# Doubling the K and V items of a streaming decode kernel to 4 MB, with b2 fetched late on the same queue

## The chip, the cores and the metric

The kernel runs on one core of one Trainium2 chip. PE is its matrix engine, ACT and DVE its scalar and vector engines, and SP issues the DMAs of the stream. SBUF is the on-chip memory, in 128 partitions; PSUM is where PE's results land. 16 DMA engines share each load; a packet is one contiguous run that one of them moves, in the trace's records. The metric is device microseconds of one execution; lower is better. Executions of one kernel agree within about 0.1% here. Ratios are the mean time of one kernel's fast runs over that of the other's of the same rounds, so they are not quite the ratios of the medians that stand beside them.

## The reference

One decode step (one query token, batch 2) of a block with adaptive layer norm: a modulation from `c`, grouped-query attention over a cache of 32768 rows, and an MLP. Cut to what matters:

```
mod = silu(c) @ w_mod                       # w_mod 1024 x 6144
h = layernorm(x) * (1 + ca) + sa
q = h @ wq                                  # 32 heads of 128, 4 KV heads, so 8 heads share one K and V
p = softmax(q @ k.T * 128**-0.5)            # k_cache, v_cache: 2 x 4 x 32768 x 128 bf16, 64 MiB each
x = x + ga * ((p @ v) @ wo)
h = layernorm(x) * (1 + cb) + sb
x = x + gb * (gelu(layernorm(h) @ w1 + b1) @ w2 + b2)
```

Everything is bf16 in memory. K and V are 134 of the 178 MB that have to be read. (The sizes of items and runs below are counted in powers of two: an item of 2 MB is 2048 KB.)

## The kernel before

All large inputs form one list of items, in the order of use, and one queue (SP's) fetches them into a ring of 160 KB a partition. An item is issued once what lay in its place has been read.

```python
CH_ROWS = 8192                 # rows of K or V in an item: 64 rows of 256 B a partition
TPC = CH_ROWS // 128
VLAG = 5                       # V item n is fetched after K item n + 5
RING = 160 * 1024
...
    b1T = sb("b1T", [128, FT])
    b2T = sb("b2T", [128, KT8])             # 8 fp32: 32 bytes a partition
    sgT = sb("sgT", [128, 2, KT8])
    ...                                     # more small tensors, S_sb, E_sb, KT_sb
    arena = nc.alloc_sbuf_tensor("arena", [128, RING], mybir.dt.uint8)
    abase = nc.lookup_mloc(arena).addr
    ...
        off = stream[-1].off + stream[-1].nbytes      # in add(): the next place in the ring
        if off + nbytes > RING:
            off = 0
    ...
    def kv_src(cache, i, cc):
        ...
        return cache[b, g][r0:r0 + CH_ROWS, :].rearrange("(p t) d -> p t d", p=128)
    ...                                     # in need(): one load an item, on SP's queue
            T.dma("sp", lambda e, dst=dst, src=cur.src: e.dma_start(dst, src), key=f"d_{cur.reg}", writes=[cur.reg], frees=old)
```

For each K item, PE transposes 128x128 tiles, ACT and DVE copy them out of PSUM, PE multiplies them with q; after the last K item of a head group comes the softmax, and PE multiplies V five items late. b2 is fetched at the start on ACT's queue, transposed into `b2T` and used near the end.

## Time and profile before

The median is 431.4 us. The page, in cut form: the span; then the 40 slices' DMA share (tenths) and rate; then the DMA queues with packets, MB and share of the 16 engines' span; then the chain of waits by engine.

```profile
span 429.7 us, 12974 instructions
...
DMA  8999999999999999999999999999999999999992
GB/s 332 432 422 426 433 432 424 432 424 427 427 432 427 426 433 429 427 433 426 426 432 426 430 433 424 429 432 426 429 429 428 430 429 424 435 424 424 427 386 112
...
q1 hardware_dynamic: 14112, 178.27, 97.6%
q8 instruction: 47, 0.77, 0.6%
...
DMA 70%; PE 24%; ACT 2%; DVE 2%; issue 1%; SPq 1%; ACTq 0%
```

DMA is busy everywhere, at 422 to 435 GB/s from the second slice to the third from the end. PE has time to spare, as the waits view shows (engine, its work, what it waited for: us in total, times, longest):

```profile
PE psKT L546 <- DMA K<-in_A_k_cache_dram: 54.2, 19, 7.5
PE psO L473 <- DMA V<-in_A_v_cache_dram: 9.5, 5, 3.0
```

The end of the stream, in the windows view (stretch and its length, busy time of PE, PE's weight loads, DVE, ACT, POOL, then the granted clock, the DMA share and GB/s):

```profile
414.00:416.00 2.00, 1.10 (x42) 1.02 (x39) 0.00 (x0) 0.00 (x0) 0.00 (x0) 0.50 1.00 422
416.00:418.00 2.00, 0.00 (x0) 0.00 (x0) 0.00 (x0) 0.00 (x0) 0.00 (x0) 0.50 0.76 315
418.00:420.00 2.00, 1.84 (x64) 1.79 (x64) 0.00 (x0) 0.00 (x0) 0.00 (x0) 0.50 0.51 209
422.00:424.00 2.00, 0.69 (x26) 0.70 (x27) 0.00 (x0) 0.00 (x0) 0.00 (x0) 0.50 0.46 193
```

From 418 us the DMA share is 0.5: about half of the DMA engines still have something to move. One load is finished when all engines have counted up its semaphore, and the trace has each count: the first load's counts are 0.4 us apart, the last w2's 9.0 us (416.68 to 425.69). Some engines fall behind during the run, and the stream ends with the slowest. What follows the last landing is short (timeline view: start, duration, engine, line, operation, and in brackets the idle time before it):

```profile
425.74 1.01 PE L591 MATMUL psS<-gT,w 128*128 128x2 bf16 x32 [0.56 <-DMA w<-in_B_w_dram]
427.90 0.37 SPq L603 DMA_DIRECT2D out_dram<-res  x1
```

Durations of single packets on the stream's queue, from the trace's DMA records (these are my own counts over them):

| packet, bytes | used for | packets an engine | median, ns |
|---|---|---|---|
| 7168 | w1 | 64 | 272 |
| 8192 | wq, w2 | 120 | 309 |
| 12288 | w_mod | 64 | 460 |
| 16384 | K, V, wo | 544 | 611 |

That makes 792 data packets an engine.

### The profile page before, as it was taken

The page shows a single profiled execution, that of the slowest core. Times are in us where ns is not written, and L with a number is a line of the kernel's source. Part 1 is how long each engine was busy: PE and PEld are TensorE (multiplying, and loading weights), DVE is VectorE, ACT ScalarE, POOL GpSimd, SP SyncE. Part 2 cuts the span into 40 slices and gives each one's busy share as a digit, 9 for nine tenths or more (in the row PEclk, how much of TensorE's full clock was granted, in tenths as well). Part 3 has the DMA queues.
Part 4 walks back from the last instruction along what each step waited for, and adds up shares of the span by engine and source line. Part 5 has one row for each costly group of instructions (what it writes and reads, how often), then busy time and mean ns, then how long its engine had stood idle before and what let it go on. Part 6 is the DMA issues. An engine that isn't in the chain of part 4 may idle for free.

```text
span 429.7 us, 12974 instructions
## 1 busy us (share of the span) xinstructions
PE 292.2 (68%) x6035; PEld 258.2 (60%) x6035; DVE 162.5 (38%) x344; ACT 158.9 (37%) x266; POOL 1.3 (0%) x9
## 2 busy tenths in 40 slices
PE   0643379859978764997877649777777697535553
PEld 0632379858867663896757548667666585203543
DVE  0200027545665332463543435445434454203200
ACT  1100016575574325362833534446436343500100
POOL 1000000000000000000000000000000000000000
PEclk9999999998989867696996959986988599555555
DMA  8999999999999999999999999999999999999992
GB/s 332 432 422 426 433 432 424 432 424 427 427 432 427 426 433 429 427 433 426 426 432 426 430 433 424 429 432 426 429 429 428 430 429 424 435 424 424 427 386 112
DMA packets 14500, 179.11 MB, mean 417 GB/s; under 512 B 1767, under 2 KB 1774, under 8 KB 2798
## 3 DMA queue, kind: packets, MB, share of 16 engines
q1 hardware_dynamic: 14112, 178.27, 97.6%
q8 instruction: 47, 0.77, 0.6%
q10 hardware_dynamic: 334, 0.02, 0.1%
q14 instruction: 7, 0.06, 0.0%
HBM read 178.28 MB, written 0.00 MB: 415 GB/s over the span
## 4 chain that ended last, share of the span: by engine, by line
DMA 70%; PE 24%; ACT 2%; DVE 2%; issue 1%; SPq 1%; ACTq 0%
DMA K<-in_A_k_cache_dram 50%; PE psKT L546 15%; DMA V<-in_A_v_cache_dram 9%; DMA w<-in_B_w_dram 7%; DMA wmod<-in_w_mod_dram 5%; PE psS L441 4%; PE psO L473 2%; PE psM L510 1%; ACT E_sb L462 1%; SPq L344 1%; PE psM L494 0%; DVE KT_sb L552 0%; PE psM L483 0%; ACT L462 0%; DVE msum L488 0%
## 5 line engine op out<-in xcount | busy, mean ns | idle before, releaser
L546 PE MATMUL psKT<-ident,K 128*128 128x128 bf16 x2048 | 181.1, 240 | 55.1 <-DMA K<-in_A_k_cache_dram 54.2
L546 PEld LDWEIGHTS psKT<-ident,K 128*128 128x128 bf16 x2048 | 138.2, 108 | 70.0 <-DMA K<-in_A_k_cache_dram 63.5
L550 ACT ACTIVATE KT_sb<-psKT 128x1024 bf16<-128x1024 bf16 x96 | 98.3, 1024 | 190.2 <-PE psKT L546 181.3
L552 DVE COPY KT_sb<-psKT 128x1024 bf16<-128x1024 bf16 x160 | 108.2, 689 | 137.7 <-PE psKT L546 137.0
L441 PE MATMUL psS<-qT,KT_sb 128*128 128x8 bf16 x2048 | 91.6, 168 | 7.2 <-ACT KT_sb L550 4.5
L441 PEld LDWEIGHTS psS<-qT,KT_sb 128*128 128x128 bf16 x2048 | 84.0, 100 | 8.6 <-ACT KT_sb L550 4.9
L473 PE MATMUL psO<-V,E_sb 128*32 128x512 bf16 x512 | 38.2, 424 | 10.1 <-DMA V<-in_A_v_cache_dram 9.5
L462 ACT ACTIVATE E_sb<-S_sb,negm 128x256 bf16<-128x256 f32 x64 | 32.5, 508 | 7.0 <-DVE negm L460 5.2
L447 DVE TENSOR_REDUCE m1c<-S_sb 128x8 f32<-128x512 f32 x32 | 22.0, 688 | 14.1 <-ACT S_sb L446 13.0
L473 PEld LDWEIGHTS psO<-V,E_sb 128*32 128x32 bf16 x512 | 11.5, 101 | 22.3 <-DMA V<-in_A_v_cache_dram 13.3
L446 ACT ACTIVATE S_sb<-psS 128x512 f32<-128x512 f32 x32 | 19.0, 594 | 4.4 <-PE psS L441 4.3
L418 PE MATMUL psS<-siluT,wmod 128*128 128x2 bf16 x384 | 11.2, 165 | 8.4 <-DMA wmod<-in_w_mod_dram 6.9
L418 PEld LDWEIGHTS psS<-siluT,wmod 128*128 128x128 bf16 x384 | 10.9, 104 | 8.8 <-DMA wmod<-in_w_mod_dram 7.3
L426 PE MATMUL psS<-hT,wq 128*128 128x2 bf16 x256 | 7.5, 165 | 12.5 <-DMA wq<-in_A_wq_dram 12.5
L426 PEld LDWEIGHTS psS<-hT,wq 128*128 128x128 bf16 x256 | 7.1, 104 | 12.8 <-DMA wq<-in_A_wq_dram 12.8
L591 PE MATMUL psS<-gT,w 128*128 128x2 bf16 x224 | 6.6, 165 | 9.2 <-DMA w<-in_B_w_dram 9.2
L395 ACT ACTIVATE stat<-stat 128x2 f32<-128x2 f32 x3 | 0.6, 203 | 31.8 <-DVE stat L394 31.8
L591 PEld LDWEIGHTS psS<-gT,w 128*128 128x128 bf16 x224 | 6.3, 104 | 9.5 <-DMA w<-in_B_w_dram 9.5
L462 ACT ACTIVATION_READ_ACCUMULATOR E_sb<-S_sb,negm 128x1 f32 x64 | 12.0, 187 | 0.0
L485 DVE RECIPROCAL rinv<-psM 128x1 f32<-128x1 f32 x8 | 1.3, 168 | 22.1 <-PE psM L483 22.1
L573 PE MATMUL psS<-h2T,w 128*128 128x2 bf16 x224 | 7.8, 172 | 2.5 <-DVE x1b L577 1.3
L573 PEld LDWEIGHTS psS<-h2T,w 128*128 128x128 bf16 x224 | 7.6, 118 | 2.6 <-issue 2.6
(86 smaller groups left out, 93.3 us busy)
## 6 DMA issues: line engine op xcount, KB each, us to landing
K<-in_A_k_cache_dram SPq DMA_DIRECT2D x32, 2048.0 KB, 44.2
V<-in_A_v_cache_dram SPq DMA_DIRECT2D x32, 2048.0 KB, 43.2
wmod<-in_w_mod_dram SPq DMA_DIRECT2D x8, 1536.0 KB, 17.2
wq<-in_A_wq_dram SPq DMA_DIRECT2D x4, 2048.0 KB, 37.7
wo<-in_A_wo_dram SPq DMA_DIRECT2D x4, 2048.0 KB, 43.0
w<-in_B_w_dram SPq DMA_DIRECT2D x4, 1792.0 KB, 41.8
w<-in_B_w_dram SPq DMA_DIRECT2D x3, 2048.0 KB, 31.0
w<-in_B_w_dram SPq DMA_DIRECT2D x1, 1024.0 KB, 29.4
```

The source lines that it names most:

```text
L418: pe(lambda e, w=it.view, j=j, k=k: e.matmul(psS[0][:, 2 * j:2 * j + 2], lhsT=w[:, j * 128:(j + 1) * 128], rhs=siluT[:, :, k], start=(k == ...
L426: pe(lambda e, w=it.view, h=h, k=k: e.matmul(psS[1][:, 2 * h:2 * h + 2], lhsT=w[:, k % 2, h * 128:(h + 1) * 128], rhs=hT[:, k, :], start=( ...
L441: pe(lambda e, t=t, jj=jj: e.matmul(ps[:, t * HPG:(t + 1) * HPG], lhsT=KT_sb[kn][:, jj, :], rhs=qT[:, b, g * HPG:(g + 1) * HPG], start=Tru ...
L446: act(lambda e: e.activation(Sc, ps[:, :].rearrange("p (t h) -> p h t", h=HPG), ACT.Copy), reads=[preg], writes=[f"S_sb{i % 2}_{cc}"])
L447: dve(lambda e: e.tensor_reduce(m1c[:, :, cc], Sc, AX.X, ALU.max), reads=[f"S_sb{i % 2}_{cc}"], writes=[f"m1c{cc}"])
L462: act(lambda e, h=h: e.activation(E_sb[j][:, :, h, :], S_sb[j][:, h, :].rearrange("p (u t) -> p u t", t=4), ACT.Exp, bias=negm[j][:, h:h + ...
L473: pe(lambda e, t4=t4, tg=tg, q=q: e.matmul(psO[32 * q:32 * q + 32, :], lhsT=E_sb[j][:, tg // 4, :, :].rearrange("p h t -> p (h t)"), rhs=i ...
L546: pe(lambda e, kq=kq, jj=jj, w=it.view, t=t: e.transpose(psKT[kq][:, jj * 128:(jj + 1) * 128], w[:, t, :], ident[:, :]), reads=[it.reg, "i ...
L550: act(lambda e, kn=kn, src=src: e.activation(KT_sb[kn][:, :, :], src, ACT.Copy), reads=[f"psKT{kq}"], writes=[f"KT_sb{kn}"])
L552: dve(lambda e, kn=kn, src=src: e.tensor_copy(KT_sb[kn][:, :, :], src), reads=[f"psKT{kq}"], writes=[f"KT_sb{kn}"])
L573: pe(lambda e, w=it.view, fc=fc, q=q, j=j, k=k: e.matmul(psS[0][:, 2 * fc:2 * fc + 2], lhsT=w[:, k % 2, q * 512 + j:(q + 1) * 512:4], rhs= ...
L591: pe(lambda e, w=it.view, q=q, j=j, k=k: e.matmul(psS[1][:, 2 * k:2 * k + 2], lhsT=w[:, q % 2, j * DM + k * 128:j * DM + (k + 1) * 128], r ...
```

## The change

The intent is fewer and larger transfers: a partition's share of a K or V item becomes one run of 32 KB, in half as many loads. To keep PSUM and the softmax as they were, the bookkeeping goes by half items. Separately, b2 leaves the head of the kernel and comes just before the last w2 item.

```diff
-CH_ROWS = 8192
+CH_ROWS = 16384
...
-VLAG = 5
+VLAG = 2
...
-    b2T = sb("b2T", [128, KT8])
...
-    T.dma("act", lambda e: e.dma_start(b2m[:, :], B_b2.rearrange("(k p) -> k p", p=128)), key="ld_b2", writes=["b2m"])
...     (the b2 matmul at the head and its copy into b2T go; qk() counts in half items)
+    need("w2", 2)
+    T.dma("sp", lambda e: e.dma_start(b2m[:, :], B_b2.rearrange("(k p) -> k p", p=128)), key="ld_b2", writes=["b2m"])
+    need("w2", 3)
     for q in range(7):
         it = need("w2", q // 2)
+        if q == 6:
+            pe(lambda e: e.matmul(psM[:, 44:52], lhsT=b2m[:, :], rhs=ident[0:KT8, 0:KT8], start=True, stop=True), ...)
+            dve(lambda e: e.tensor_tensor(x1b[:, :, :], mod(5), psM[:, 44:52].unsqueeze(2).to_broadcast([128, KT8, 2]), ALU.mult), ...)
+            dve(lambda e: e.tensor_tensor(x1b[:, :, :], x1b[:, :, :], x1T[:, :, :], ALU.add), ...)
```

More of the change, by code (lines that the diff above doesn't have):

```diff
@@ L30 @@
 NK = NBG * NCH
-VLAG = 5
+STEPS = TPC // 8
+VLAG = 2
 NKT = 6
@@ L263, in bass_adaLN_cond__gqa_block_cached__mixer_channel_mlp__decode_kernel @@
     res16 = sb("res16", [16, 128], BF16)
-    m1c = sb("m1c", [128, HPG, NCH])
+    m1c = sb("m1c", [128, HPG, NT // 64])
     m1 = sb("m1", [128, HPG])
@@ L375, in bass_adaLN_cond__gqa_block_cached__mixer_channel_mlp__decode_kernel @@
         pe(lambda e, j=j: e.matmul(psM[:, 16 + 7 * j:23 + 7 * j], lhsT=b1m[:, j::4], rhs=ident[0:7, 0:7], start=True, stop=True),
-           reads=["b1m", "ident"], writes=["psM"], mark=False)
-    pe(lambda e: e.matmul(psM[:, 44:52], lhsT=b2m[:, :], rhs=ident[0:KT8, 0:KT8], start=True, stop=True),
-       reads=["b2m", "ident"], writes=["psM"])
+           reads=["b1m", "ident"], writes=["psM"], mark=(j == 3))
     dve(lambda e: e.tensor_copy(xT.rearrange("p k b -> p b k"), psM[:, 0:16].rearrange("p (b k) -> p b k", b=2)), reads=["psM"], writes=["xT"])
     dve(lambda e: e.tensor_copy(b1T.rearrange("p (q j) -> p j q", j=4), psM[:, 16:44].rearrange("p (j q) -> p j q", j=4)), reads=["psM"], writes=["b1T"])
-    dve(lambda e: e.tensor_copy(b2T[:, :], psM[:, 44:52]), reads=["psM"], writes=["b2T"])
     def kb(ap2):
@@ L437, in qk @@
         b, g = i % 2, i // 2
-        ps, preg = psS[n % 2], f"psS{n % 2}"
+        hh, half = cc * (TPC // 64) + g8 // 8, (g8 // 8) % 2
+        ps, preg = psS[half], f"psS{half}"
         for jj in range(8):
-            t = g8 * 8 + jj
+            t = (g8 % 8) * 8 + jj
             pe(lambda e, t=t, jj=jj: e.matmul(ps[:, t * HPG:(t + 1) * HPG], lhsT=KT_sb[kn][:, jj, :], rhs=qT[:, b, g * HPG:(g + 1) * HPG],
@@ L443, in qk @@
                reads=[f"KT_sb{kn}", "qT"], writes=[preg], mark=(jj == 7))
-        if g8 == TPC // 8 - 1:
-            Sc = S_sb[i % 2][:, :, cc * TPC:(cc + 1) * TPC]
-            act(lambda e: e.activation(Sc, ps[:, :].rearrange("p (t h) -> p h t", h=HPG), ACT.Copy), reads=[preg], writes=[f"S_sb{i % 2}_{cc}"])
-            dve(lambda e: e.tensor_reduce(m1c[:, :, cc], Sc, AX.X, ALU.max), reads=[f"S_sb{i % 2}_{cc}"], writes=[f"m1c{cc}"])
+        if g8 % 8 == 7:
+            Sc = S_sb[i % 2][:, :, hh * 64:(hh + 1) * 64]
+            act(lambda e: e.activation(Sc, ps[:, :].rearrange("p (t h) -> p h t", h=HPG), ACT.Copy), reads=[preg], writes=[f"S_sb{i % 2}_{hh}"])
+            dve(lambda e: e.tensor_reduce(m1c[:, :, hh], Sc, AX.X, ALU.max), reads=[f"S_sb{i % 2}_{hh}"], writes=[f"m1c{hh}"])
     def softmax_1(i):
-        dve(lambda e: e.tensor_reduce(m1[:, :], m1c[:, :, :], AX.X, ALU.max), reads=[f"m1c{cc}" for cc in range(NCH)], writes=["m1"])
+        dve(lambda e: e.tensor_reduce(m1[:, :], m1c[:, :, :], AX.X, ALU.max), reads=[f"m1c{hh}" for hh in range(NT // 64)], writes=["m1"])
     def softmax_2(i):
@@ L463, in softmax_3 @@
                                             accum_out=rowsum[j][:, h:h + 1]),
-                reads=[f"S_sb{j}_{cc}" for cc in range(NCH)] + [f"negm{j}"], writes=[f"E_sb{j}", f"rowsum{j}"])
+                reads=[f"S_sb{j}_{hh}" for hh in range(NT // 64)] + [f"negm{j}"], writes=[f"E_sb{j}", f"rowsum{j}"])
     def pv(v):
@@ L536, in bass_adaLN_cond__gqa_block_cached__mixer_channel_mlp__decode_kernel @@
     for n in range(NK + VLAG + 1):
-        for g8 in range(TPC // 8):
+        for g8 in range(STEPS):
             if n < NK:
@@ L576, in bass_adaLN_cond__gqa_block_cached__mixer_channel_mlp__decode_kernel @@
                reads=[it.reg, "h2T"], writes=["psS0"], mark=(fc == FT - 1))
-    dve(lambda e: e.tensor_tensor(x1b[:, :, :], mod(5), b2T[:, :].unsqueeze(2).to_broadcast([128, KT8, 2]), ALU.mult), reads=["modT", "b2T"], writes=["x1b"])
-    dve(lambda e: e.tensor_tensor(x1b[:, :, :], x1b[:, :, :], x1T[:, :, :], ALU.add), reads=["x1b", "x1T"], writes=["x1b"])
     dve(lambda e: e.tensor_tensor(zT[:, :, :], psS[0][:, 0:2 * FT].rearrange("p (f b) -> p f b", b=2), b1T[:, :].unsqueeze(2).to_broadcast([128, FT, 2]), ALU.add),
@@ L585, in bass_adaLN_cond__gqa_block_cached__mixer_channel_mlp__decode_kernel @@
     dve(lambda e: e.tensor_tensor(gT[:, :, :], sg[:, :, :], zT[:, :, :], ALU.mult), reads=["sg", "zT"], writes=["gT"])
+    need("w2", 2)
+    T.dma("sp", lambda e: e.dma_start(b2m[:, :], B_b2.rearrange("(k p) -> k p", p=128)), key="ld_b2", writes=["b2m"])
+    need("w2", 3)
     for q in range(7):
         it = need("w2", q // 2)
+        if q == 6:
+            pe(lambda e: e.matmul(psM[:, 44:52], lhsT=b2m[:, :], rhs=ident[0:KT8, 0:KT8], start=True, stop=True),
+               reads=["b2m", "ident"], writes=["psM"])
+            dve(lambda e: e.tensor_tensor(x1b[:, :, :], mod(5), psM[:, 44:52].unsqueeze(2).to_broadcast([128, KT8, 2]), ALU.mult),
+                reads=["modT", "psM"], writes=["x1b"])
+            dve(lambda e: e.tensor_tensor(x1b[:, :, :], x1b[:, :, :], x1T[:, :, :], ALU.add), reads=["x1b", "x1T"], writes=["x1b"])
         for j in range(4):
```

## The prediction

> **What bounds the kernel now.** The DMA stream. The page's slices show the 16 DMA engines at 9 tenths and 422 to 435 GB/s from the second slice to the 38th; the chain of waits is 70% DMA. PE is busy 68% and waits 54.2 us for K and 9.5 us for V (waits view), so it has some 64 us to spare. The Trainium skill, "DMA: Bandwidth & Descriptors", Specifications, puts the fabric ceiling at 435 GB/s; this trace's steady 428 agrees, so at most 1.6% is left in mid-stream.
>
> The stream is never short of work: by the trace's issues and landings, when a K or V item is issued the load before it still has over 20 us to run.
>
> Bandwidth is lost in the tail: from 417 to 425 us the DMA share is 0.5 (windows view), 205 to 221 GB/s. The 16 semaphore increments of one load are spread over 0.4 us at the start and 9.0 us at the end, widening by about 1.4 us with each batch of 16 KB instruction-fetch packets (47 in all, queue 8). Half of the engines lag and finish alone. The last w2 lands at 425.7; 4 us of PE, DVE and output follow.
>
> **Removed.** 32 of 64 K/V issues, off the critical path. Half of the K/V packets: each engine's 512 packets of 16 KB become 256 of 32 KB. A packet of 8192 bytes took 309 ns, one of 16384 bytes 611, so about 7 ns do not scale; the spacing of landings (4.86 us an item of eight packets an engine, 4.88 for sixteen half as large) says 3 to 5. Estimate: 256 x 3 to 7 ns, plus 32 semaphore packets of 9 ns: 1 to 2 us, all critical. At the head the b2 fetch, its matmul and a DVE copy: PE's first wmod matmul (15.65) starts up to 1 us earlier, hidden under DMA.
>
> **Added.** A 2 KB load before the last w2: some 25 ns on a few engines. One small matmul and two DVE operations of 0.17 us, hidden in the wait for the last w2. A PV of twice the length after the last V, 1.9 us more at half clock: w1 begins later, but the end still waits for w2.
>
> **Moved.** Buffers come free in 32 KB steps: five slots instead of ten, four and a half with a wo in the ring. Estimate from this trace's K-item times (5.1 to 11.1 us per 64 tiles): the backlog at an issue falls from over 20 us to 7 at the worst; DMA should not run dry. It would with PE 25 to 30% slower. PE's waits get fewer and longer; its granted clock may shift. The 47 fetches and the half-idle tail stay.
>
> **Predicted:** 430.1 us, 80% range 427.8 to 433.0; faster by over 2% 0.03, within 2% 0.90, slower by over 2% 0.07.
>
> **Right if:** 16 KB packets become 32 KB ones near 1215 to 1218 ns; mid-stream slices stay at 424 to 436 GB/s; the tail is still 8 to 9 us of half the engines; the last w2 lands 1 to 2 us earlier, and 4 us follow.
>
> **Wrong if:** 32 KB packets are split (no gain); engines reading partitions 128 KB apart collide in memory (the same page's "HBM row pitch at large powers of two" shows loss at far larger pitches; no run here shows it); the ring runs dry (slices below 415 GB/s); or instruction fetches cost more behind 32 KB packets, or fall on other engines, moving the tail by 1.4 us a packet.

## More of the kernel before

SBUF tensors are laid one after another, so the ring starts where the small tensors end. In this kernel the build puts it at byte 61440 of a partition, a multiple of 256 (and of 4096). Every offset inside the ring is a multiple of 256 too.

## The result and the profile after

The changed kernel takes 433.45 us (433.36 to 433.69, four runs) against 431.44 for the kernel before: ratio 1.0047, 95% interval 1.003 to 1.0065. It is slower by 2.0 us, a small but certain difference, and 0.45 us outside the predicted range. The same lines of its page:

```profile
span 431.7 us, 12947 instructions
...
DMA  8999999999999999999999999999999999999992
GB/s 331 431 416 417 440 433 433 419 424 428 427 433 428 411 437 434 433 421 428 424 427 430 437 430 427 418 422 436 436 419 436 429 423 399 428 408 417 418 397 111
...
q1 hardware_dynamic: 9520, 178.27, 97.2%
q8 instruction: 47, 0.77, 0.7%
...
DMA 57%; PE 27%; ACT 8%; DVE 4%; SPq 2%; issue 1%; DVEq 0%; ACTq 0%
```

The packets of the stream fell from 14112 to 9520, so the 32 KB runs were not split, and DMA is still busy to the end. Yet it did not gain. DMA's share of the chain fell to 57%, with more PE and ACT in it; I read that as PE working through longer items between two waits. It is no sign of a new limit, as the faster kernel below has the same 57%. The tail has the same form, only later:

```profile
416.00:418.00 2.00, 1.17 (x44) 1.08 (x41) 0.00 (x0) 0.00 (x0) 0.00 (x0) 0.50 1.01 418
420.00:422.00 2.00, 1.69 (x63) 1.69 (x64) 0.00 (x0) 0.00 (x0) 0.00 (x0) 0.50 0.52 209
424.00:426.00 2.00, 0.75 (x28) 0.75 (x29) 0.00 (x0) 0.00 (x0) 0.00 (x0) 0.50 0.46 189
```

Here is b2's new place, and the end:

```profile
427.05 0.18 PE L588 MATMUL psM<-ident,b2m 8*128 8x8 bf16 x1
427.27 0.17 DVE L590 TENSOR_TENSOR x1b<-modT,psM 128x16 f32<-128x16 f32 x1 [13.33 <-PE psM L588]
427.48 0.17 DVE L592 TENSOR_TENSOR x1b<-x1b,x1T 128x16 f32<-128x16 f32 x1
427.74 1.01 PE L595 MATMUL psS<-gT,w 128*128 128x2 bf16 x32 [0.51 <-DMA w<-in_B_w_dram]
429.91 0.35 SPq L607 DMA_DIRECT2D out_dram<-res  x1
```

The b2 matmul and the two DVE operations are done before the last w2 has landed (PE then idles 0.51 us for it), so b2 is off the critical path, as predicted. From the last block of 32 matmuls to the issue of the output it is 2.17 us, before 2.16. The whole loss therefore lies in the stream: its last landing moved from 425.69 to 427.70, 2.01 us.

Where in the stream? Counted at the slowest engine, the landing of the last wq, which comes before any K or V and which the change did not touch, had already moved from 53.41 to 54.27 us. From there to the last wo the time grew by 0.77 us, where it should have shrunk, and in the MLP weights, again untouched, by 0.38 us. A loss that is spread over loads which the change leaves alone points at something common to all loads. The packet records show it:

| packet, bytes | before, median ns | after, median ns |
|---|---|---|
| 7168 | 272 | 275 |
| 8192 | 309 | 313 |
| 12288 | 460 | 464 |
| 16384 | 611 | 614 |
| 32768 | none | 1216 |

Every packet has become 3 to 4 ns longer, whatever its size. All the packets have one thing in common: they are written into the ring. Removing `b2T` took 32 bytes out of the tensors ahead of it, and the build now places the ring at byte 61408, which is 224 past a multiple of 256.

### The profile page after: what moved, and what is told of

Its sections match the earlier page's. It is cut to its first block, busy times and chain, and to the rows that moved or that the text cites. A ratio compares the mean times of both kernels' runs of the same rounds, so it can differ in the third digit from the quotient of the medians.

```text
span 431.7 us, 12947 instructions
## 1 busy us (share of the span) xinstructions
PE 291.8 (68%) x6035; PEld 259.5 (60%) x6035; DVE 161.3 (37%) x343; ACT 157.1 (36%) x266; POOL 1.3 (0%) x9
## 3 DMA queue, kind: packets, MB, share of 16 engines
q1 hardware_dynamic: 9520, 178.27, 97.2%
## 4 chain that ended last, share of the span: by engine, by line
DMA 57%; PE 27%; ACT 8%; DVE 4%; SPq 2%; issue 1%; DVEq 0%; ACTq 0%
DMA K<-in_A_k_cache_dram 46%; PE psKT L543 16%; ACT E_sb L459 7%; DMA w<-in_B_w_dram 6%; DMA wmod<-in_w_mod_dram 5%; PE psS L438 4%; PE psO L470 2%; DVE KT_sb L549 2%; SPq L344 2%; PE psM L507 1%; ACT KT_sb L547 1%; PE psM L491 1%; PE psM L480 1%; DVE msum L485 1%; PE psM L450 1%
## 5 line engine op out<-in xcount | busy, mean ns | idle before, releaser
L470 PEld LDWEIGHTS psO<-V,E_sb 128*32 128x32 bf16 x512 | 14.4, 112 | 22.9 <-issue 15.8
L485 DVE SCALAR_TENSOR_TENSOR msum<-psO,mk,msum 128x128 f32<-128x128 f32 x24 | 8.4, 351 | 0.9
```

The source lines that it names most:

```text
L470: pe(lambda e, t4=t4, tg=tg, q=q: e.matmul(psO[32 * q:32 * q + 32, :], lhsT=E_sb[j][:, tg // 4, :, :].rearrange("p h t -> p (h t)"), rhs=i ...
```

## The experiments

Theory A: the displaced start of the ring makes each packet longer, and the change without that would have gained. Theory B: the large items cost time themselves (dearer instruction fetches behind 32 KB packets, a ring that comes free in large steps). Theory C: b2 in the stream costs time. The first four kernels separate the three causes.

### after_pad32: the changed kernel, ring back in place

```diff
+    pad = nc.alloc_sbuf_tensor("pad", [128, 32], mybir.dt.uint8)
     arena = nc.alloc_sbuf_tensor("arena", [128, RING], mybir.dt.uint8)
```

> The changed kernel with a 32-byte dummy tensor ahead of the ring, so that the ring starts at byte 61440 of a partition again (as in the kernel before) and not at 61408, where the removal of b2T had moved it. Theory A (start of the ring): packets of 8192 bytes go back from 313 to 309 ns, of 32768 bytes from 1216 to about 1211; some 536 packets an engine times 4 ns, so about 2 us less than the changed kernel: 431.0 to 431.8. Theory B (large items cost time themselves, through instruction fetches and a ring that frees late): stays at 433.0 to 433.7. Theory C (b2 in the stream): stays at 433.0 to 433.7.

Measured: 430.09 us (430.0 to 430.1, five runs), 3.36 us faster than the changed kernel as handed over and 1.3 us faster than before: ratio 0.9968, interval 0.9955 to 0.9982. Packets of 8192 bytes are back at 309 ns, those of 32768 bytes at 1213. Theory A holds, with a larger effect than the 2 us expected (the time lies below its range). All the other small tensors stayed where the change had put them, so it is the ring alone.

```profile
span 428.2 us, 12947 instructions
...
GB/s 329 430 425 424 444 439 436 425 419 427 435 435 433 415 441 429 436 433 422 431 434 418 441 433 430 427 435 436 424 419 436 435 438 402 422 419 422 427 410 111
...
DMA 57%; PE 26%; ACT 8%; DVE 4%; SPq 2%; issue 2%; DVEq 0%; ACTq 0%
```

This is the version that beats both: all of the change with one dummy of 32 bytes.

### before_pad224: the kernel before, ring displaced

```diff
+    pad = nc.alloc_sbuf_tensor("pad", [128, 224], mybir.dt.uint8)
     arena = nc.alloc_sbuf_tensor("arena", [128, RING], mybir.dt.uint8)
```

> The kernel before with a dummy tensor of 224 bytes ahead of the ring, so that the ring starts at 61664, 224 past a multiple of 256 as in the changed kernel; nothing else is changed. Theory A: packets of 16384 bytes take 614 to 615 ns instead of 611; 792 packets an engine times 4 ns, 3 us more than before: 434.0 to 435.0. Theories B and C: as before, 431.3 to 431.7.

Measured: 436.20 us, ratio 1.0111, interval 1.0097 to 1.0124. A dummy that nobody reads costs 4.8 us, again more than expected. The expectation had taken 4 ns a packet from the medians; the mean 16 KB packet grew by 4.7 ns (613.6 to 618.3) and the time by 6.1 ns for each of 792 packets. With 536 packets, in the changed kernel, it was 6.3. In before_pad224 not all of it is in the data packets: the first engine to finish counts the last w2 at 420.87 us instead of 416.68, which is 4.2 us or 5.3 ns a packet, and the other 0.6 us is a wider spread of the counts (9.6 us instead of 9.0). The instruction packets on queue 8, here 1066 ns on average instead of 945, fit that part, but no run isolates it. The page shows the loss as a lower rate through the whole run, on average 424 GB/s in the second to the 38th slice, where the kernel before has 428:

```profile
GB/s 333 425 419 418 425 427 425 419 422 431 418 425 425 425 427 422 427 424 422 425 424 422 427 428 418 424 430 427 421 425 422 429 421 422 430 417 419 416 370 111
```

### after_small and after_small_pad32: b2 moved, items of 2 MB

```diff
-CH_ROWS = 16384
+CH_ROWS = 8192
-VLAG = 2
+VLAG = 5
-        hh, half = cc * (TPC // 64) + g8 // 8, (g8 // 8) % 2
+        hh, half = cc * (TPC // 64) + g8 // 8, n % 2
```

The second has the 32-byte dummy as well.

> The changed kernel with items of 2 MB and a lag of 5 again; b2 stays late in the stream and the ring stays at 61408. Theory A: the misplaced start costs 792 packets an engine, not 536, so slower than the changed kernel by about 1 us less what large items cost: 433.5 to 435.0, as the kernel before with its ring moved. Theory B: back to about 431.5. Theory C: 433 to 433.7.

> The changed kernel with items of 2 MB, b2 late in the stream, and the ring back at 61440: against the kernel before only b2 has moved. Theory A: 431.2 to 431.7, as before. Theory B: 431.2 to 431.7 too. Theory C: about 433.5. Against the changed kernel with the ring back at 61440 it says what large items are worth by themselves.

Measured: 436.17 us without the dummy and 431.43 with it (ratio 1.0, interval 0.9987 to 1.0012). So moving b2 is worth nothing that can be measured here, and theory C falls. after_small equals before_pad224, which has b2 early: 4.7 us over its kernel with the ring in place, dearer than expected because the price of a packet was. Theory B falls as well: with the ring displaced, large items are faster by 2.7 us (436.17 to 433.45), with the ring in place by 1.3 us (431.43 to 430.09). The large items were never the cost. They reduced the damage, because there are fewer packets to pay for.

### large_two_runs: large items of small packets

What did the large items gain by? This kernel is after_pad32 with each partition of an item filled by two runs of 16 KB.

```diff
-        return cache[b, g][r0:r0 + CH_ROWS, :].rearrange("(p t) d -> p t d", p=128)
+        return cache[b, g][r0:r0 + CH_ROWS, :].rearrange("(h p t) d -> p h (t d)", h=2, p=128)
...     (the destination is split into the same two runs)
```

> The changed kernel with the ring back at 61440 and items of 4 MB, but each partition of an item filled by two runs of 16 KB instead of one of 32 KB: packets as of before, issues, semaphores and freeing as of the large items. If the 1.3 us that large items gain lie in the number of packets: 431.2 to 431.6. If they lie in the number of loads and semaphores, or in the schedule: 430.0 to 430.3.

Measured: 431.24 us. The gain of 1.34 us over after_small_pad32 thus splits into 1.15 for the halved packets and 0.19 for everything else about large items, which is too little to tell from nothing (the interval of the ratio is 0.13% to each side, some 0.5 us). The spacing of the landings agrees: the first engine to finish counts an item of 4 MB every 9.72 us in two loads of the kernel before (2 x 4.862), every 9.72 here, every 9.67 with runs of 32 KB (medians).

### before_pad32, before_pad128, before_pad256, before_pad64: how the start counts

Each is the kernel before with a dummy of that many bytes ahead of the ring, as above.

The Trainium skill, "DMA: Bandwidth & Descriptors", section "How a descriptor splits into AXI transactions", says that a descriptor is split into transactions of 256 bytes, in beats of 32, and that one which does not start at a 256-byte boundary also fetches the bytes from the boundary below, which cost beats. It speaks of bytes that are fetched; that the same holds for a destination in SBUF was my assumption. By that rule, as an estimate, a packet of 16 KB takes 512 beats from an aligned start, 513 from 32 past, 516 from 128 past and 519 from 224 past. That gave numbers to test.

> The kernel before with a dummy of 32 bytes ahead of the ring: it starts 32 past a multiple of 256. Three forms of theory A. A1 (beats[...]): one seventh of the 4.8 us of the 224-byte dummy, so 431.9 to 432.4. A2 (a fixed price for any start off a multiple of 256, for one more transaction): 436. A3 (only the place within 64 bytes counts): 436.

> The same with a dummy of 128 bytes: the ring starts 128 past a multiple of 256. A1 (516 beats, four sevenths of 4.8 us): 433.7 to 434.5. A2 (fixed price): 436. A3 (64 bytes count): 431.4.

> The same with a dummy of 256 bytes: a ring that has moved but starts at a multiple of 256. All forms of theory A: 431.3 to 431.6, as before, packets of 16384 bytes at 611 ns. If it is slower, it is the move or the dummy, not the alignment.

> The kernel before with its ring 64 past a multiple of 256. The 128-byte dummy cost 3.6 us and the 32- and 224-byte ones 4.7. If the cost has a first part for any start off a multiple of 256 (3.6 us) and a second for a start off a multiple of 64 (1.1 us): 435.0 to 435.2. If it falls evenly with the start's largest power of two (32: 4.7, 64: about 4.2, 128: 3.6): 435.5 to 435.8. If only 128 is special: 436.1.

| ring starts past a multiple of 256 by | median, us | over the kernel before, us | the same divided by 792 packets, ns | mean 16 KB packet, ns |
|---|---|---|---|---|
| 0 (as before) | 431.4 | | | 613.6 |
| 0 (dummy of 256) | 431.48 | 0.0 | 0 | 613.6 |
| 32 | 436.14 | 4.7 | 5.9 | 618.3 |
| 64 | 435.36 | 4.0 | 5.0 | 617.3 |
| 128 | 435.07 | 3.6 | 4.6 | 616.9 |
| 224 | 436.20 | 4.8 | 6.1 | 618.3 |

A dummy of 256 bytes is free, so it is neither the dummy nor the move but the start's place within 256 bytes. The counting of beats fails for this destination: 32 past costs as much as 224 past, where it should have been a seventh. Most of the price (3.6 of 4.8 us) is due at any of the starts tried off the boundary; a start 32 bytes past a multiple of 64 pays about 1 us more (0.7 to 1.2). The start at 64 came out between the first two of its three forecasts and decides between neither. Why there is a fixed price (one transaction more for each packet would fit) and whether it arises on the side that writes SBUF was not tested: only the destination moved here, but nothing in these runs looks inside a transfer.

### before_more_fetch: where the half-idle tail comes from

The prediction blamed the tail on instruction fetches. This kernel is the one before, with half of the QK matmuls issued twice.

```diff
-        for jj in range(8):
+        for jj in (0, 1, 2, 3, 0, 1, 2, 3, 4, 5, 6, 7):
```

> The kernel before with its ring in place, where half of the QK matmuls are issued twice: 1024 more matmuls and as many weight loads, about 128 KB or 8 more packets of instruction fetch; some 25 us more of PE time, which PE has. If the half-idle tail comes from instruction fetches: 55 packets instead of 47, a seventh step of about 1.4 us in the spread of the landings (10.3 us at the end instead of 9.0), and 432.6 to 433.0. If the spread has another origin: 431.4 and a spread of 9.0.

Measured: 432.74 us, ratio 1.003, interval 1.0016 to 1.0043, with the eight fetches more that were expected:

```profile
q8 instruction: 55, 0.90, 0.7%
```

The counts of the last w2 are now 10.1 us apart (416.85 to 426.98) instead of 9.0: the first engines end where they did, the last 1.3 us later, and so does the kernel. PE still had time to spare. Here a batch of eight 16 KB instruction packets costs 1.3 us of the end.

## Why the prediction was wrong, and where it was right

The mechanism that the prediction forecast was right and so was its size: with the ring in place the change gains 1.34 us, where 1 to 2 were forecast. That it then takes 430.09 us and the prediction said 430.1 is in part luck: the range was 5 us wide, and the short gap of the quick engines and the narrower tail (below) were not foreseen. It was still wrong for the kernel as it was handed over, because a term was missing. The sum, from the medians:

| step | us | shown by |
|---|---|---|
| before | 431.4 | |
| b2 late | 0.0 | after_small_pad32 |
| large items, without their longer runs | -0.2 (not clear of noise) | large_two_runs |
| runs of 32 KB, half of the K/V packets | -1.15 | after_pad32 |
| ring at 61408 instead of 61440 | +3.36 | the changed kernel against after_pad32 |
| after | 433.45 | |

- The step that failed is "Removed". It lists issues, packets and the work on b2 at the head, and leaves out that the diff also removes `b2T` from the row of SBUF tensors. Nothing in the listed work is wrong; what was missed is where the remaining tensors then lie. In its place the runs showed a cost of 3.36 us: the ring moved from byte 61440 to 61408, and every load of the stream, untouched ones included, paid for it (6.3 ns for each of 536 packets an engine). "Wrong if" named four dangers (split packets, collisions in memory, a dry ring, dearer fetches), and none about the place in SBUF that a load is written to. The fetches did get dearer in the changed kernel (1066 ns instead of 945), but not from standing behind 32 KB packets: with the ring in place they took 932.
- "1 to 2 us, all critical" for the packets and semaphores: 1.34 us with the ring in place.
- "Near 1215 to 1218 ns": 1213 in place. The changed kernel's 1216 lies inside the forecast although it contains the penalty, so that line alone would have seemed to confirm the prediction. The 8192-byte packets, which the change does not touch, gave it away.
- "The backlog falls to 7 us at the worst; DMA should not run dry": with the ring in place the worst issue of a K or V item came 6.6 us ahead for the slowest engine, at 190 us, but only 0.4 us ahead for the quickest, at 356 us. The quickest engines had a short gap there (their landings are 10.9 us apart, elsewhere 9.67), and a slice fell to 402 GB/s (changed kernel: 399), under the mark of 415 that the prediction had set as a sign of failure. That mark was misjudged: the gap is on engines that are ahead by over 7 us and stand idle at the end. large_two_runs, with the same large steps of freeing, loses nothing against after_small_pad32. (The page counts a packet's bytes in the slice in which it starts, so slices with 32 KB packets scatter more; with the bytes spread over each packet's time, by my count, this slice has 407 GB/s and its neighbours 425 and 426.)
- "The 47 fetches and the half-idle tail stay": 47 packets, and the tail is there, with counts 7.4 us apart after instead of 9.0. That the fetches cause it, then argued, is now supported by before_more_fetch: eight more of them added one step of the forecast size. That the spread shrank because the quick engines ran dry fits their landings (a gap of 1.2 us), but no run isolates it.
- The danger "HBM row pitch at large powers of two" (the Trainium skill, "DMA: Bandwidth & Descriptors", "Latency and other measured facts") did not appear at a pitch of 32 KB: the 32 KB packets ran at 27.0 bytes a ns, those of 16 KB at 26.8.
- b2: hidden at both ends, as predicted.

## What to carry to other kernels

When a diff adds or removes a tensor, look at where the large DMA destinations start afterwards: here 32 bytes cost 3.4 us, more than the change had to give, and each of the four starts tried off a multiple of 256 cost 3.6 to 4.8 us in the kernel before. Pin such a buffer at a multiple of 256 by a pad ahead of it, and check the address that the build gives (`abase % 256` here) whenever small tensors come or go. To allocate it first is not enough by itself: in a build of the kernel before with the ring allocated first (built only, not run) it starts at byte 16512, which is 128 past a multiple of 256. And when a kernel bound by DMA is slower everywhere, compare the durations of packets that the change did not touch before explaining the ones that it did.

## What the Trainium skill lacked or had wrong

- "DMA: Bandwidth & Descriptors", "How a descriptor splits into AXI transactions": it speaks of bytes fetched and does not say what the start of a destination costs. For one in SBUF 256-byte boundaries matter too (a destination moved by 256 bytes cost 0.0 us, by 128 bytes 3.6), but the count of beats doesn't give the price: 32 bytes past the boundary cost 5.9 ns a packet, 224 past 6.1, 64 past 5.0 and 128 past 4.6, where the extra beats by that rule, as an estimate, would go as 1, 7, 2 and 4.
- "SBUF — State Buffer", "Operand start alignment": it says of element-aligned starts, DMAs' included, that "This is about legality, not speed", and no page gives a rule of speed for the start of a DMA destination. Here a start 32, 64, 128 or 224 bytes past a multiple of 256 cost 0.8 to 1.1% of a kernel bound by DMA.
- "DMA: Bandwidth & Descriptors", "Rules for kernel authors", asks for at least 1 MiB a DMA. Every large load of both kernels is at or above that, and what still gained was the length of a partition's run, not the size of the DMA: 4 MB in runs of 16 KB took 431.24 us, in runs of 32 KB 430.09.
- No page says what instruction fetch costs a data stream beside it (it would belong in "Runtime: NRT & Kernel Launch", "Instruction fetch mechanics"): with 47 packets of 16 KB the landings were spread over 9.0 us at the end, and eight more cost 1.3 us. In the runs with a displaced ring these packets took about 1070 ns on average instead of 929 to 945, though nothing had moved their own destination; that stays unexplained.
